# Key-value products of two batches in one group, with k read as loaded, in a fused attention and feed-forward kernel

## The chip, the core and the metric

The kernel runs on one core of a Trainium2 chip. The metric is the device time of one execution in microseconds (us), as the median of several runs. Beside it stands one profiled execution, whose trace gives the start and length of every instruction on the engines (PE for matrix products, PEld for its weight loads, DVE for vector work, ACT for scalar work, POOL and SP, which here mostly issue transfers) and the traffic of the core's 16 DMA engines.

## What is computed

Eight batches of eight heads, 576 tokens each, head width 64. The first half is linear attention without a softmax, with a norm per token and head; the second a feed-forward layer over all 4608 tokens with a PReLU between two products. Cut to its core:

```python
kv  = np.einsum('bhsd,bhse->bhde', k, v)
out = np.einsum('bhsd,bhde->bhse', q, kv)
rms = np.sqrt(np.mean(out * out, axis=-1, keepdims=True) + 1e-06)
x   = (out / rms * g_norm)            # to [4608, 512]
h = x @ w_in                          # [512, 2048]
g = np.maximum(h, 0.0) + alpha * np.minimum(h, 0.0)
return (g @ w_out)                    # [2048, 512]
```

The change is in `kv`: for each batch and head the 64 x 64 product of k and v, summed over the 576 tokens.

## The kernel before

The 4608 tokens are worked through in nine windows of 512 (W = 512, NW = 9). A batch has 576 tokens, so a window and a batch do not coincide: window 4 needs the end of batch 3 and the start of batch 4. The order of instructions on PE, ACT, DVE, POOL and SP is written out by hand; every engine takes its instructions in that order.

The loop at line 1056 runs over w from 1 to 8, and in it over 16 units u. One unit issues the four products of one 128-column block of the feed-forward layer for window w (`m1_group`, line 523; the group of u = 0 is split by `m1_cols` into the first 384 tokens and the last 128 for w >= 3), seven products of the second layer for window w - 1 (`prod_mm`, line 656), and a step of the attention for window w + 1 (`attention`, line 1032). So the attention of a window runs one window ahead of its use.

What the attention of window w + 1 consists of, from w = 2 on: `row_kv` (line 994) makes the key-value products of batch w + 1, at u = 2 for w = 2 and at u = 0 later, as 4 head pairs x 5 token groups x 2 heads = 40 small products into `kv_ps`, and two ACT casts put them into `kv_masked`. `rows_mm` (line 439), one unit later, multiplies the transposed q (`qt_sb`) by `kv_masked`. Then square, sum, root and norm follow for four blocks of 128 tokens (ACT, DVE), and after each norm SP issues a DMA transpose of the 128 normed tokens into `xt` (line 492), the feed-forward input of the next window. The norms of the four blocks come at u = 5, 7, 9, 12 for w = 2 and at u = 3, 6, 8, 11 later. SP also issues five DMA transposes per batch for q (`dma_t`, line 356, into `qt_sb`), at u = 8, 10, 12 or 7, 9, 11.

The loads of k, v and q turn fp32 in memory into fp16 on the core. They are issued by POOL, in one queue. Tokens 0 to 511 of a batch go into stage tiles (`load_main`, line 165, for k and v; `load_q`, line 173), with two stage tiles each for k and v in turn; the last 64 tokens go straight into `bufs` (`load_rem`, line 185), with three of those for k and v. `load_gated(w + 2)` (line 204) stands at the start of each w up to 5 and issues nine loads for batch w + 2: q rest, k rest, k, four for q, v rest, v. The batch is used one w later. The first of them, q rest, waits on POOL until the last DMA transpose of the batch before has read the buffer that it overwrites. Behind the loads in POOL's queue stand stores of finished output (line 550).

The products read v as it was loaded, `stages[b, "v"][:, head, t, :]`, but k from `bufs`, where `regroup` (line 191) has copied it from [head, token group, d] into [token group, head, d]. For batches 4 to 7 ACT does it, in four pieces at u = 9, 11, 13, 15 (`REG_AT`), and for batch 3 in two ACT pieces and one DVE piece at w = 2, u = 0.

`row_tile` (line 72) hands out two tiles of two PSUM banks each in turn, which `kv_ps` and the two `or_ps` of a window share.

Of the kernel before, what the change touches and what calls it, by code (L numbers as in the profile page):

```python
# [10 lines left out]
FP16 = mybir.dt.float16  # L11
# [6 lines left out]
def kernel(  # L18
# [11 lines left out]
    nc = tc.nc  # L30

    B, H, S, D = q.shape
# [3 lines left out]
    P = 128  # L36
    NPAIR = H // 2
# [3 lines left out]
    TPP = S // P  # L41
    MAIN = TPP * P
    REM = S - MAIN
    NT = TPP + 1
# [27 lines left out]
    def row_tile(shape, name):  # L72
        if not row_pool:
            early.close()
            row_pool.append(
                ctx.enter_context(tc.tile_pool(name="psr", bufs=2, space=bass.MemoryType.PSUM))
            )
        t = row_pool[0].tile([P, 2, W], FP32, name=name, tag="r")
        n = 1
        for x in shape:  # L80
            n *= x
        flat = t[:].rearrange("p b n -> p (b n)")[:, 0:n]
        names = [f"x{i}" for i in range(len(shape))]
        return flat.rearrange(
            f"p ({' '.join(names)}) -> p {' '.join(names)}", **dict(zip(names, shape))
        )
# [78 lines left out]
    def load_main(b, nm, h0=0, h1=H):  # L165
        if (b, nm) not in stages:
            stages[b, nm] = stage_p.tile([P, H, TPP, D], FP16, name=f"{nm}st", tag=f"{nm}st")
        nc.gpsimd.dma_start(
            out=stages[b, nm][:, h0:h1].rearrange("p h t d -> p h (t d)"),
            in_=srcs[nm][b, h0:h1, 0:MAIN, :].rearrange("h (p t) d -> p h (t d)", t=TPP),  # L170
        )
# [10 lines left out]
    def buf_of(b, nm):  # L182
        return bufs[min(b, B_NAT) % 2 if nm == "q" else b % NBUF][nm]

    def load_rem(b, nm):
        nc.gpsimd.dma_start(
            out=buf_of(b, nm)[0:REM, 0 if nm == "v" else TPP, :, :],
            in_=srcs[nm][b, :, MAIN:S, :].rearrange("h s d -> s h d"),
        )

    def regroup(b, nm, h0, h1, eng=None):
        dst = buf_of(b, nm)[:, 0:TPP, h0:h1, :].rearrange("p t h d -> p h t d")
        src = stages[b, nm][:, h0:h1, :, :]
        if eng is nc.scalar:
            nc.scalar.copy(out=dst, in_=src)
        else:
            (eng or nc.vector).tensor_copy(out=dst, in_=src)
# [6 lines left out]
    def load_gated(b):  # L204
        load_rem(b, "q")
        if b == B_NAT:
            load_q(b)
        load_rem(b, "k")
        load_main(b, "k")
        if b > B_NAT:  # L210
            load_q(b)
        load_rem(b, "v")
        load_main(b, "v")

    def regroup0(nm, j, n=1):
        i, h = divmod(2 * j, HH)
# [1 line left out]
            out=bufs[0][nm][0:P0, :, 2 * j : 2 * (j + n), :].rearrange("p t h d -> p h t d"),  # L218
            in_=stages[0, nm, i][0:P0, h : h + 2 * n],
        )  # L220

    def regroup_pair(b, nm, j):
        regroup(b, nm, 2 * j, 2 * j + 2, nc.scalar)


    WQ = 4
    w_in_sb = []
# [72 lines left out]


    qts, kvs, xts = {}, {}, {}
    kv_masked = [const_p.tile([P, NPAIR, P], FP16, name=f"kv_masked{i}") for i in range(2)]

    def rows(b):
        return P0 if b == 0 else P
# [1 line left out]
    def n_runs(b):  # L308
        return T0 if b == 0 else NT

    def pair_cols(b, nm, j):
        def f(t):
            n = rows(b)
            if nm == "v" and b == 0:
                h = 2 * j % HH
                return stages[b, nm, 2 * j // HH][0:n, h : h + 2, t, :]
            if nm == "v" and t < TPP:
                return stages[b, nm][:, 2 * j : 2 * j + 2, t, :]
            if nm == "v":
                return buf_of(b, nm)[0:n, 0, 2 * j : 2 * j + 2, :]  # L320
            return buf_of(b, nm)[0:n, t, 2 * j : 2 * j + 2, :]
        return f
# [44 lines left out]
    def step_kv(b, j, pool=(ps_s, "s")):  # L367
        ks, vs = pair_cols(b, "k", j), pair_cols(b, "v", j)
        kv_ps = pool[0].tile([P, P], FP32, name="kv_ps", tag=pool[1])
        for t in range(n_runs(b)):  # L370
            nc.tensor.matmul(  # L371
                out=kv_ps[:],
                lhsT=ks(t),
                rhs=vs(t),
                start=(t == 0),
                stop=(t == n_runs(b) - 1),
            )
        kvs[b, j] = kv_masked[b % 2][:, j, :]
        nc.vector.tensor_mul(out=kvs[b, j], in0=kv_ps[:], in1=mask32[:])


# [609 lines left out]
            ATT_1.setdefault(at, []).append((what, j))  # L991
    ATT = {"t": step_t, "kv": step_kv, "ot": step_ot, "ssq": step_ssq}

    def row_kv(b):
        kv_ps = row_tile([NPAIR, D], "kv_ps")
        for j in range(NPAIR):
            ks, vs = pair_cols(b, "k", j), pair_cols(b, "v", j)
            for t in range(n_runs(b)):
                for i in range(2):
                    rows_i = slice(i * D, (i + 1) * D)  # L1000
                    nc.tensor.matmul(  # L1001
                        out=kv_ps[rows_i, j, :], lhsT=ks(t)[:, i, :], rhs=vs(t)[:, i, :],
                        start=(t == 0), stop=(t == n_runs(b) - 1), skip_group_check=True,
                    )
        for i in range(2):
            rows_i = slice(i * D, (i + 1) * D)
            nc.scalar.copy(out=kv_masked[b % 2][rows_i, :, rows_i], in_=kv_ps[rows_i, :, :])
        for j in range(NPAIR):
            kvs[b, j] = kv_masked[b % 2][:, j, :]

    ATT_ROW = {}
    ROW_AT = {
        True: dict(
# [18 lines left out]
    def attention(w, u):  # L1032
        if W_ROW <= w < NW:
            for what, j in ATT_ROW[w == W_ROW].get(u, ()):
                if what != "kv":
                    ROWS[what](w, j)
                elif w < B:
                    row_kv(w)
            if w + 1 < B:
                dma_t(w + 1, QT_AT[w == W_ROW].get(u, ()))  # L1040
        elif w < NW:
            for what, j in (ATT_1 if w == 2 else ATT_AT).get(u, ()):
                if what == "t" and w >= B_NAT:
                    continue
                if w < B or what in ("ot", "ssq"):
                    if w == 2 and what in ("kv", "ssq"):
                        pool = Q_POOL if j % 2 == 0 else S_POOL
                        (step_kv if what == "kv" else step_ssq)(w, j, pool)
                    else:
                        ATT[what](w, j)  # L1050

    REG_AT = {9 + 2 * j: (("k", j),) for j in range(NPAIR)}

    Y3_AT = [(13, 13), (13, 13), (13, 13), (13, 14), (14, 14), (14, 15), (15, 15), (15, 15), (15, 15), (15, 15), (15, 15), (15, 15), (15, 15), (15, 15), (15, 16), (16, 16)]

    for w in range(1, NW):
        if w + 2 < B:
            load_gated(w + 2)
        for u in range(NF):
            if w >= W_ROW - 1 and u in R_FIRST:  # L1060
                y_read(w - 1, R_FIRST[u])
            late = w >= W_ROW and u == 0
            if late:
                h_ps = h_bank()
                m1_cols(h_ps, w, G_ORDER[u], 0, W - P)
            else:
                m1_group(w, G_ORDER[u])
            if w < 3 and (w, u) in ((1, NF - 1), (2, 0)):
                s_sum(1, w, 2)
            if w == W_ROW - 1:  # L1070
                scale_w_in(G_ORDER[u])
            if w > 1:
                unit_sums(w, u)
            if w == 1 and u == 1:
                regroup(2, "k", 0, H)
            if w == 2 and u == 0:
                h_tags[0] = ("h1", "h2")
                h_turn[0] = 0
            if w > 2 and u == 0 and not late:
                y_read(w - 2, "c12")  # L1080
            if w == 1:
                for i in range(*Y3_AT[u]):
                    y_mm(ys[3], 0, 3, i)
                    if i == NF - 1:
                        y_out(ys[3], 0, 3)
            else:
                for i in range(u * PER, (u + 1) * PER):
                    prod_mm(w - 1, *Y_LIST[i])
                    if late and i == 3:
                        m1_cols(h_ps, w, G_ORDER[u], W - P, W)  # L1090
                        y_read(w - 2, "c12")
                        m1_evac(h_ps, w, G_ORDER[u])
                for what in (R_ROW if w >= W_ROW - 1 else Y_READS).get(u, ()):
                    y_read(w - 1, what)
            attention(w + 1, u)
            if w == 1 and u == 12:
                dma_t(3, (3, 4, 0, 1, 2))
            if w == 1:
                for k in {5: (0,), 7: (1,)}.get(u, ()):
                    s_sum(1, 1, k)  # L1100
                    s_sum(1, 2, k)
            if w + 2 < B:
                for nm, j in REG_AT.get(u, ()) if w > 1 else ():
                    regroup_pair(w + 2, nm, j)
            if w == 2:
                if u == 0:
                    regroup_pair(3, "k", 0)
                    regroup_pair(3, "k", 1)
                    regroup(3, "k", HH, H)
    w = NW - 1  # L1110
    store_engines[0] = (nc.sync, nc.scalar)
    Y_READS[13] = Y_READS.pop(14)
# [54 lines left out]
```

## Time and profile before

| | |
|---|---|
| median of 3 runs | 274.97 us (273.76 to 275.08) |
| the profiled execution | 275.59 us |
| its span in the trace | 273.6 us |
| mean granted TensorE clock | 0.994 |
| PE busy | 266.3 us, 97% of the span |
| DVE busy | 227.9 us, 83% |
| ACT busy | 155.9 us, 57% |
| POOL busy | 86.2 us, 32% |
| software DMA queue (POOL's), share of 16 engines | 69.5% |
| hardware DMA queue (SP's transposes and stores), share | 17.1% |

The span is cut in the page into 40 slices of 6.84 us. A digit there is the busy share of a slice in tenths, where 9 stands for 90% or more. The time from issue to landing of a transfer is measured from the start of the instruction that issues it.

### The profile page before, as it was taken

The numbers are of one execution on the slowest core, as the hardware profiler recorded it, in microseconds if no ns is written. First come the engines' busy times: TensorE is split into PE (matmuls) and PEld (weight loads), VectorE is DVE, ScalarE is ACT, GpSimd is POOL, SyncE is SP. The second block draws the span as 40 slices with busy tenths as digits, with TensorE's granted clock in tenths as the row PEclk, the third lists the DMA queues.
The fourth block names the chain that finished last, engine by engine and source line by source line (L and its number), as shares of the span: only waits on it lengthen the run. The fifth ranks groups of instructions, "written<-read, shape, count | busy, mean of one in ns | idle before, by whom it ended". The sixth has DMA issues, their size and how long they took to land.

```text
span 273.6 us, 5687 instructions
## 1 busy us (share of the span) xinstructions
PE 266.3 (97%) x2181; PEld 170.8 (62%) x2181; DVE 227.9 (83%) x432; ACT 155.9 (57%) x294; POOL 86.2 (32%) x123
## 2 busy tenths in 40 slices
PE   7799999999999999999999999999999999999995
PEld 2364464555666766666666666666666666666794
DVE  6459938899889979997999799979998999877863
ACT  3267555879989865645565556555544553443210
POOL 8773462780733355226421551100110012000200
PEclk9799999999999999999999999999999999999999
DMA  8999999999999689966996699720222122201223
GB/s 161 196 200 199 197 202 189 220 112 162 137 164 180 99 129 149 170 153 113 155 167 147 112 156 164 151 89 19 77 60 77 22 77 60 77 1 41 77 79 116
DMA packets 87343, 34.56 MB, mean 126 GB/s; under 512 B 58884, under 2 KB 85652, under 8 KB 87316
## 3 DMA queue, kind: packets, MB, share of 16 engines
q0 software_dynamic: 58064, 24.35, 69.5%
q1 hardware_dynamic: 28212, 8.83, 17.1%
q10 hardware_dynamic: 1040, 1.02, 1.2%
q8 instruction: 17, 0.28, 0.4%
q14 instruction: 10, 0.08, 0.1%
HBM read 36.71 MB, written 9.44 MB: 169 GB/s over the span
## 4 chain that ended last, share of the span: by engine, by line
PE 95%; DMA 2%; DVE 1%; issue 0%; ACT 0%; POOLq 0%
PE h_ps L507 43%; PE yY L688 15%; PE yX L688 10%; PE yZ L688 10%; PE y L539 5%; DMA vst<-in_v_dram 2%; PE h_ps L530 2%; PE kv_ps L371 2%; PE or_ps L452 1%; PE kv_ps L1001 1%; PE ssq_ps L416 1%; PE qt_ps L327 1%; PE ot_ps L393 1%; PE yZ L683 1%; PE warm_ps L295 0%
## 5 line engine op out<-in xcount | busy, mean ns | idle before, releaser
L507 PE MATMUL h_ps<-xt,w_in_sb 128*128 128x512 f16 x544 | 136.9, 379 | 0.0
L514 ACT ACTIVATE m_sb<-h_ps 128x512 f32<-128x512 f32 x144 | 86.1, 599 | 78.1 <-PE h_ps L507 67.7
L518 DVE SCALAR_TENSOR_TENSOR gt<-m_sb,beta_sb,h_ps 128x512 f16<-128x512 f32 x144 | 106.2, 744 | 24.1 <-ACT m_sb L514 22.5
L507 PEld LDWEIGHTS <-w_in_sb 128*128 128x128 f16 x544 | 52.1, 98 | 40.0
L550 POOL DMA_DIRECT2D out_dram<-y_sb x36 | 22.6, 630 | 134.3 <-ACT y_sb L726 53.4
L688 PEld LDWEIGHTS <-s 128*128 128x128 f16 x496 | 48.5, 98 | 19.1
L688 PEld LDWEIGHTS <-gt 128*128 128x128 f16 x384 | 37.3, 98 | 14.0
L688 PE MATMUL yY<-wsum,s 128*128 128x256 f16 x256 | 36.3, 273 | 0.0
L688 PE MATMUL yX<-w_out_sb,gt 128*128 128x256 f16 x256 | 36.1, 273 | 0.0
L177 POOL DMA_DIRECT2D qst<-in_q_dram x20 | 17.7, 923 | 1.8 <-DMA vst<-in_v_dram 1.8
L688 PE MATMUL yY<-wsum,gt 128*128 128x256 f16 x128 | 17.6, 273 | 0.0
L688 PE MATMUL yZ<-wsum,s 128*128 128x256 f16 x120 | 16.7, 273 | 0.0
L688 PE MATMUL yZ<-w_out_sb,s 128*128 128x256 f16 x120 | 16.7, 273 | 0.0
L487 DVE TENSOR_TENSOR x_rows<-or_ps,rstd_r 128x512 f16<-128x512 f32 x24 | 16.4, 683 | 0.0
L469 DVE TENSOR_REDUCE ssq_r<-sq_sb 128x8 f32<-128x512 f16 x24 | 16.3, 678 | 0.0
L463 ACT ACTIVATE sq_sb<-or_ps 128x512 f16<-128x512 f32 x24 | 14.4, 599 | 2.6 <-PE or_ps L452 2.6
L539 PE MATMUL y<-w_out_sb,gt 128*128 128x512 f16 x64 | 15.8, 379 | 0.0
L625 DVE TENSOR_TENSOR s<-s,gt 128x512 f16<-128x512 f16 x32 | 13.5, 421 | 0.5
L623 DVE TENSOR_TENSOR s<-gt 128x512 f16<-128x512 f16 x32 | 13.4, 418 | 0.0
L629 DVE TENSOR_TENSOR s<-gt,s 128x512 f16<-128x512 f16 x32 | 13.2, 417 | 0.0
L627 DVE TENSOR_TENSOR s<-gt 128x512 f16<-128x512 f16 x32 | 13.0, 418 | 0.0
L720 DVE TENSOR_TENSOR u<-yY,p 128x512 f32<-128x512 f32 x16 | 10.9, 683 | 1.9 <-PE yY L688 1.7
(88 smaller groups left out, 249.9 us busy)
## 6 DMA issues: line engine op xcount, KB each, us to landing
out_dram<-y_sb POOLq DMA_DIRECT2D x16, 256.0 KB, 2.7
kst<-in_k_dram POOLq DMA_DIRECT2D x7, 512.0 KB, 7.9
vst<-in_v_dram POOLq DMA_DIRECT2D x6, 512.0 KB, 10.5
qst<-in_q_dram POOLq DMA_DIRECT2D x20, 128.0 KB, 8.0
w_out_sb<-in_moe_w_out_dram POOLq DMA_DIRECT2D x8, 256.0 KB, 11.7
out_dram<-y_sb SPq DMA_DIRECT2D x5, 256.0 KB, 2.2
w_in_sb<-in_moe_w_in_dram POOLq DMA_DIRECT2D x2, 512.0 KB, 10.0
qst<-in_q_dram POOLq DMA_DIRECT2D x2, 512.0 KB, 12.1
```

Of the source, the lines that this page charges most:

```text
L177: nc.gpsimd.dma_start(out=st[:, t, :, :], in_=srcs["q"][b, :, t * P : (t + 1) * P, :].rearrange("h p d -> p h d"),)
L463: nc.scalar.activation(out=sq[:], in_=o_ps, func=AF.Square)
L469: nc.vector.tensor_reduce(out=ssq[:].rearrange("p h j -> p (h j)"), in_=sq[:].rearrange("p h j d -> p (h j) d"), axis=mybir.AxisListType.X ...
L487: nc.vector.tensor_tensor(out=xr[:].rearrange("p j h d -> p h j d"), in0=o_ps, in1=rstd[:].unsqueeze(3).to_broadcast([P, 2, NPAIR, D]), op ...
L507: nc.tensor.matmul(out=h_ps[:], lhsT=w_in_blk(c, g), rhs=xts[w][:, c, :], start=(c == 0), stop=(c == NC - 1),)
L514: nc.scalar.activation(out=m_sb[:], in_=h_ps[:], func=AF.Relu, scale=-1.0)
L518: nc.vector.scalar_tensor_tensor(out=gts[w, i][:, r, :], in0=m_sb[:], scalar=beta_sb[:, g : g + 1], in1=h_ps[:], op0=ALU.mult, op1=ALU.add,)
L539: nc.tensor.matmul(out=y[:], lhsT=gt_cols(w, g, a * P, (a + 1) * P), rhs=w_out_blk(g), start=(g == 0), stop=(g == NF - 1),)
L550: engs[store_turn[0] % len(engs)].dma_start(out=dst, in_=src)
L623: nc.vector.tensor_add(out=t[:], in0=a21, in1=a22)
L625: nc.vector.tensor_sub(out=t[:], in0=sums[w, 1, k][:], in1=a11)
L688: nc.tensor.matmul(out=bank, lhsT=lhs, rhs=rhs, start=fresh, stop=(c == NK - 1), skip_group_check=True,)
```

## The change

Batch 3 stays alone; batches 4 and 5 are made in one group of 80 products, with one pair of casts, where batch 4 was made alone, and 6 and 7 likewise where batch 6 was. The k and v loads of batch 5 move from the start of w = 3 to the start of w = 2, behind those of batch 4, and those of batch 7 from w = 5 to w = 4, behind those of batch 6; the q loads stay where they are. For batches 3 to 7 the products read k from the stage tile, and the copies go. `kv_masked` has three batch slots in place of two tiles.

```diff
@@ load_gated
         load_rem(b, "q")
         if b == B_NAT:
             load_q(b)
-        load_rem(b, "k")
-        load_main(b, "k")
+        first, *more = {3: (3,), 4: (4, 5), 6: (6, 7)}.get(b, (None,))
+        if first:
+            load_rem(b, "k")
+            load_main(b, "k")
         if b > B_NAT:
             load_q(b)
-        load_rem(b, "v")
-        load_main(b, "v")
+        if first:
+            load_rem(b, "v")
+            load_main(b, "v")
+        for c in more:
+            for nm in ("k", "v"):
+                load_rem(c, nm)
+                load_main(c, nm)
@@
-    def regroup_pair(b, nm, j):
-        regroup(b, nm, 2 * j, 2 * j + 2, nc.scalar)
@@
-    kv_masked = [const_p.tile([P, NPAIR, P], FP16, name=f"kv_masked{i}") for i in range(2)]
+    kv_masked = const_p.tile([P, NBUF, NPAIR, P], FP16, name="kv_masked")
@@ step_kv
-        kvs[b, j] = kv_masked[b % 2][:, j, :]
+        kvs[b, j] = kv_masked[:, b % NBUF, j, :]
@@
-    def row_kv(b):
-        kv_ps = row_tile([NPAIR, D], "kv_ps")
-        for j in range(NPAIR):
-            ks, vs = pair_cols(b, "k", j), pair_cols(b, "v", j)
-            for t in range(n_runs(b)):
-                for i in range(2):
-                    rows_i = slice(i * D, (i + 1) * D)
-                    nc.tensor.matmul(
-                        out=kv_ps[rows_i, j, :], lhsT=ks(t)[:, i, :], rhs=vs(t)[:, i, :],
-                        start=(t == 0), stop=(t == n_runs(b) - 1), skip_group_check=True,
-                    )
+    def head_rows(b, nm, h, t):
+        if t < TPP:
+            return stages[b, nm][:, h, t, :]
+        return buf_of(b, nm)[:, t if nm == "k" else 0, h, :]
+
+    def row_kv(bs):
+        n = len(bs)
+        kv_ps = row_tile([n, NPAIR, D], "kv_ps")
+        for x, b in enumerate(bs):
+            for j in range(NPAIR):
+                for t in range(NT):
+                    for i in range(2):
+                        nc.tensor.matmul(
+                            out=kv_ps[i * D : (i + 1) * D, x, j, :],
+                            lhsT=head_rows(b, "k", 2 * j + i, t),
+                            rhs=head_rows(b, "v", 2 * j + i, t),
+                            start=(t == 0), stop=(t == NT - 1), skip_group_check=True,
+                        )
+                kvs[b, j] = kv_masked[:, b % NBUF, j, :]
+        b0 = bs[0] % NBUF
         for i in range(2):
-            rows_i = slice(i * D, (i + 1) * D)
-            nc.scalar.copy(out=kv_masked[b % 2][rows_i, :, rows_i], in_=kv_ps[rows_i, :, :])
-        for j in range(NPAIR):
-            kvs[b, j] = kv_masked[b % 2][:, j, :]
-
+            part = slice(i * D, (i + 1) * D)
+            nc.scalar.copy(out=kv_masked[part, b0 : b0 + n, :, part], in_=kv_ps[part])
+
+    KV_OF = {3: (3,), 4: (4, 5), 6: (6, 7)}
@@ attention
-                elif w < B:
-                    row_kv(w)
+                elif w in KV_OF:
+                    row_kv(KV_OF[w])
@@ the loop over w
-    REG_AT = {9 + 2 * j: (("k", j),) for j in range(NPAIR)}
...
-            if w + 2 < B:
-                for nm, j in REG_AT.get(u, ()) if w > 1 else ():
-                    regroup_pair(w + 2, nm, j)
-            if w == 2:
-                if u == 0:
-                    regroup_pair(3, "k", 0)
-                    regroup_pair(3, "k", 1)
-                    regroup(3, "k", HH, H)
```

## The prediction

> **What bounds the kernel now.** I read the page's engine shares and its chain of work first, to see which engine sets the end.
>
> ```profile
> PE 266.3 (97%) x2181; PEld 170.8 (62%) x2181; DVE 227.9 (83%) x432; ACT 155.9 (57%) x294; POOL 86.2 (32%) x123
> ...
> PE 95%; DMA 2%; DVE 1%; issue 0%; ACT 0%; POOLq 0%
> ```
>
> The chain that ends last is PE's own work for 95% of the span. Its DMA part (2%) is the wait for v of batch 0 that ends near 8 us; the change does not touch it. Next I asked whether PE runs dense in the stretch that the change touches. The timeline of PE at the turn from w = 2 to w = 3, and below it the turn from w = 6 to w = 7, where there are no key-value products left to make (columns: start us, length us, engine, line, operation, out<-in, shape, count):
>
> ```profile
> 94.48 0.81 PE L530 MATMUL h_ps<-xt,w_in_sb 128*128 128x384 f16 x4
> 95.13 0.60 PE L688 MATMUL yX<-w_out_sb,gt 128*128 128x256 f16 x4
> 95.56 0.39 PE L530 MATMUL h_ps<-xt,w_in_sb 128*128 128x128 f16 x4
> 95.79 0.49 PE L688 MATMUL yX<-w_out_sb,gt 128*128 128x256 f16 x3
> 96.21 0.32 PE L1001 MATMUL kv_ps<-vst,ksb 128*64 128x64 f16 x8
> 96.36 0.20 PE L1001 MATMUL kv_ps<-vsb,ksb 128*64 128x64 f16 x2
> ...
> 96.67 0.20 PE L1001 MATMUL kv_ps<-vsb,ksb 128*64 128x64 f16 x2
> ...
> 96.96 1.04 PE L507 MATMUL h_ps<-xt,w_in_sb 128*128 128x512 f16 x4
> ```
>
> ```profile
> 206.15 0.39 PE L530 MATMUL h_ps<-xt,w_in_sb 128*128 128x128 f16 x4
> 206.37 0.49 PE L688 MATMUL yX<-w_out_sb,gt 128*128 128x256 f16 x3
> 206.70 1.03 PE L507 MATMUL h_ps<-xt,w_in_sb 128*128 128x512 f16 x4
> ```
>
> In the chain a unit is four products of 0.86 us together and seven of 0.77 us: 1.63 us, sixteen of them 26.0 us. The windows that start at 97.03, 124.62, 152.32, 179.91 and 206.86 us last 27.6, 27.7, 27.6, 26.9 and 26.7 us: the units, the small attention products, and no gap. So nothing that ACT or DVE gives up can shorten these windows, and whatever makes PE wait lengthens the run by as much. There are two inputs that PE could wait for here: the normed tokens in `xt` (needed at 94.48 and 95.56 us) and k and v (needed at 96.21).
>
> **What the change takes off PE.** The products stay 200 in number, with the same operand shapes. The second pair ends at 96.36 + 0.20, the next a step of 0.155 us later (96.36, 96.51, 96.67), so 40 products stream in 4 x 0.155 = 0.62 us. From the last 128-column products to the next group PE takes 96.96 - 95.56 = 1.40 us with key-value products and 206.70 - 206.15 = 0.55 us without: a group costs 0.85 us, of which 0.85 - 0.62 = 0.23 us is entry and exit. Two groups fewer (those of batches 5 and 7): 2 x 0.23 = **0.46 us gained**. Bounds: nothing, if the streams do not pack as well, and 0.5.
>
> **What it takes off ACT and DVE.** 18 copies (line 195) of 611 ns, 10.9 us on ACT, and one DVE copy of 418 ns. ACT is idle for 78.1 us ahead of its own line 514 alone, mostly waiting for PE; in this stretch PE never waits for ACT. Worth **0**. If that slack were not there, the four copies of one window would be worth 2.4 us.
>
> **What it adds on ACT.** The casts of one batch take 0.37 us each (line 1007); those of two batches have twice the elements. The step from 128x256 to 128x512 in the squares (382 to 595 ns) puts 256 elements at 0.21 us, so 0.58 each and 1.16 the pair. Before, they ended at 97.82 and `rows_mm` began at 98.70. With 0.62 us more products, the casts end near 97.08 + 0.62 + 1.16 = 98.86 and `rows_mm` would begin at 99.32: hidden with 0.46 us to spare. **0**; a cover gone would cost what it is late, at most a few tenths.
>
> **What it moves: four loads.** On POOL the issues at the start of w = 2 are:
>
> ```profile
> 70.20 0.69 POOL L186 DMA_DIRECT2D qsb<-in_q_dram  x1 [9.81 <-DMA qt_sb<-qsb]
> 70.88 0.70 POOL L186 DMA_DIRECT2D ksb<-in_k_dram  x1
> 71.56 0.91 POOL L168 DMA_DIRECT2D kst<-in_k_dram  x1
> 72.43 3.54 POOL L177 DMA_DIRECT2D qst<-in_q_dram  x4
> 75.89 0.76 POOL L186 DMA_DIRECT2D vsb<-in_v_dram  x1
> 76.57 0.97 POOL L168 DMA_DIRECT2D vst<-in_v_dram  x1
> 82.85 2.16 POOL L550 DMA_DIRECT2D out_dram<-y_sb  x4 [5.32 <-ACT rstd_r L479]
> ```
>
> Behind the issue at 76.57 come k rest, k, v rest, v of batch 5: 0.70 + 0.91 + 0.76 + 0.97 = 3.3 us of issuing. At the start of the kernel POOL issued eight loads and then waited for the first to land (1.14 us, at 8.27), so the new k load waits for the third load of this batch, which lands at 71.56 + 8.4 = 79.96, and the new v load for the second q load, near 81.6. All are in the queue before v of batch 4 lands (76.57 + 10.7 = 87.27), so the DMA engines do not run dry. The stage tiles that they overwrite, of batch 3, are free at 72.5, where its products end. POOL's stores of 82.85 land later; there are four `y_sb` tiles and four are filled per window, so each has 27 us. Issuing: **0**. The later windows lose these loads, where they were hidden anyway: **0**.
>
> The transfers themselves are another matter. Between the landing of k (79.96) and that of v (87.27) the queue brought four q loads, v rest and v: 4 x 128 + 64 + 512 KB = 1.11 MB in 7.3 us, 152 GB/s. Two k and v pairs of the moved batch are 1152 KB = 1.18 MB: 7.8 us more, until 95.0, and in this time three transposes of 128 KB also want the engines (0.13 MB at 152 GB/s is 0.86 us each), 97.6 at the outside. PE needs batch 5 at 96.21 + 0.62 = 96.8. Late by **0 to 0.8 us**. At w = 4 v of batch 6 lands at 132.20 + 10.7 = 142.9; batch 7 then at 150.7 to 153.3, needed at 151.50 + 0.62 = 152.1: **0 to 1.2 us**.
>
> **What is late next: the transposes into `xt`.** They share the 16 engines with the loads. Transfers by issue, in narrow stretches, one at 109.19 while the loads of w = 3 fill the engines and one at 91.90 after those of w = 2 are through (SP's queue, microseconds to landing last):
>
> ```profile
> xt<-x_rows SPq DMA_TRANSPOSE x1, 7.8
> ```
>
> ```profile
> xt<-x_rows SPq DMA_TRANSPOSE x1, 2.5
> ```
>
> In the stretch from 78 to 82 us every digit of DMA use is 9, and the one transpose issued there (80.25) has moved no bytes by 83. So a transpose under load takes up to 7.8 us, and 2.5 without. The fourth block of w = 2 is issued at 91.90 and needed at 95.56: 94.4 without load, 99.7 at worst with it. The load lasts until some 95 to 97.6, that is for most of the flight; I take 5.5 us, a little above the middle, hence 97.4: **1.8 us late** (bounds 0 and 4.1). The kv group then begins 1.8 later and the load of batch 5 is there. The third block (issued 86.69) lands by 94.5 even at 7.8, when it is needed at 94.48. At w = 4 the fourth block is issued at 145.03 and needed at 150.85: 5.8 us of room, so late only above that (bounds 0 and 2.0); I take the load of batch 7 as the later one there, **1.0 us**, near its far bound, since transposes and loads lengthen each other.
>
> The Trainium skill's page "DMA: Bandwidth & Descriptors", section "Queues, rings and completion order", says that each DMA engine goes round robin between the queues that have work, packet by packet. By that rule a transpose would have half the engines' rate at once: 0.13 MB at half of 152 GB/s, 1.7 us in place of 0.9, some 3.4 us to landing as an estimate, and both blocks would be in time; the sum would be -0.46 us or little above. The row of 7.8 us speaks against so even a share, so I go by the row.
>
> **The sum.** -0.46 + 1.8 + 1.0 = +2.34 us on the profiled execution's 275.59 (a span of 273.6 and 2.0 around it): 277.9. The median of the runs shown is 0.6 below that execution, so 277.3 for the median. Bounds: -0.46, and -0.46 + 4.1 + 2.0 = +5.6.
>
> **The rivals.** *All of it is hidden.* The place is the same, the fourth block's transpose and the moved loads. For it: v loads alone ran at 195 to 209 GB/s (82 to 84 us), and between 84 and 96 us the engines were idle for some 6.2 us by the digits of their use. At 200 GB/s the load takes 5.9 us and is through at 93.2; a transpose that lands within 3.7 us of its issue at 91.90, and 5.8 at 145.03, costs nothing. Then only the 0.46 us remains: 274.97 - 0.46 = 274.5, not slower. It decides from that 3.7 us. Against it: those issued while the engines were full took 5.2 to 7.8 us. *A backlog.* Transposes go through one queue in order; at w = 4 those issued at 136.90, 138.18, 140.15 and 141.44 all landed between 144.1 and 145.8, some 3 us after the loads of that window were through at about 142. If that repeats behind a load that lasts until 97.6, the third block of w = 2 lands at 100.6, 6.1 us after 94.48, and w = 4 adds 2.0: with the 0.46 off, +7.6, 282.6. For it: that bunching. Against it: under load the ones of 132.01 and 109.19 came through in 7.1 and 7.8 us, before the load ended. *The pairing helps PE more than I count*, by over 0.5%: that needs 1.4 us off PE, three times the entry and exit of both groups; I see no row for it.
>
> **How the numbers follow.** About 0.5%, 1.4 us, is what a measurement of this kernel can tell from no change. Forecast (late by 1.4 to 5.6 us): 0.50, its own range 276.3 to 280.6. All hidden or nearly: 0.37. Backlog: 0.10. More gain: 0.03. So slower 0.60, same 0.37, faster 0.03. The range has to take in the hidden case: 274.2 to 280.6, which leaves out the backlog and little below.
>
> **What would show it.** In the trace after: PE idle ahead of line 530 at w = 3, u = 0 (about 1.8 us, released by the transpose into `xt`), and ahead of the kv group at w = 5 (about 1 us, released by the load into the v or k stage tile); transposes issued near 92 and 145 us with landings of 5 us and more; the software queue at full use until about 95 and 151 us; two kv groups of about 1.45 us and none at two window starts; windows of 26.7 us without. I am wrong if PE has no gaps there, if line 452 waits for the casts, or if the gap is over 4 us.

## The result

| | before | after |
|---|---|---|
| median of 6 runs each | 274.68 us (273.76 to 275.37) | 289.11 us (286.86 to 290.06) |
| ratio, with its 95% interval | | 1.052 (1.047 to 1.056) |
| the profiled execution, its span | 275.59, 273.6 us | 289.28, 287.4 us |
| mean granted TensorE clock | 0.994 | 0.976 |

The change costs 14.4 us, where 2.3 was forecast. One of the experiments below (one pair, even loads) has runs in two groups 4 us apart; they are given one by one there.

The page of the changed kernel, engine shares, the slices of PE and its clock, and the chain of work that ended last:

```profile
PE 269.5 (94%) x2181; PEld 172.7 (60%) x2181; DVE 228.1 (79%) x431; ACT 146.6 (51%) x272; POOL 86.5 (30%) x123
...
PE   7799999999999399999998299999999999999995
...
PEclk9999999999999869999999699999999999999999
...
PE 87%; DMA 7%; DVE 3%; ACT 1%; issue 1%; DVEq 0%
```

Two slices of PE now read 3 and 2 (a slice is 7.2 us here). The clock reads 8 in the first of them and 6 in the slice behind it, and 6 in the second. DMA's part of the chain has risen from 2% to 7%; the page's list by line gives nearly all of it to `xt<-x_rows`, SP's transposes. The PE timeline at the two turns (lines are 3 higher than before at `m1_cols`, so 533 is the old 530; in brackets the idle time ahead and what ended it):

```profile
94.59 0.81 PE L533 MATMUL h_ps<-xt,w_in_sb 128*128 128x384 f16 x4 [1.46 <-DMA xt<-x_rows]
...
99.47 0.58 PE L533 MATMUL h_ps<-xt,w_in_sb 128*128 128x128 f16 x4 [3.63 <-DMA xt<-x_rows]
99.85 0.84 PE L691 MATMUL yX<-w_out_sb,gt 128*128 128x256 f16 x3
100.62 0.43 PE L1009 MATMUL kv_ps<-vst,kst 128*64 128x64 f16 x8
100.86 0.25 PE L1009 MATMUL kv_ps<-vsb,ksb 128*64 128x64 f16 x2
100.91 0.41 PE L1009 MATMUL kv_ps<-vst,kst 128*64 128x64 f16 x8
...
157.01 0.82 PE L533 MATMUL h_ps<-xt,w_in_sb 128*128 128x384 f16 x4 [0.94 <-DMA xt<-x_rows]
...
163.69 0.59 PE L533 MATMUL h_ps<-xt,w_in_sb 128*128 128x128 f16 x4 [5.41 <-DMA xt<-x_rows]
```

PE waits for the first three blocks (1.46 and 0.94 us) and again for the fourth (3.63 and 5.41): 5.1 us at the first turn, 6.35 at the second, all of it released by a transpose into `xt`. Line 1009 has no idle time ahead of it: PE does not wait for k or v. But its pairs of heads come 100.91 - 100.62 = 0.29 and then 0.27 us apart, where it was 0.155 before. The granted clock by stretches of 2 us shows why (columns: PE, PEld, DVE, ACT, POOL busy with instructions, then the clock, DMA share, GB/s):

```profile
96.00:98.00 2.00, 0.00 (x0) 0.00 (x0) 0.00 (x0) 0.00 (x0) 0.68 (x2) 1.00 1.29 212
98.00:100.00 2.00, 0.53 (x5) 0.53 (x5) 0.00 (x0) 0.00 (x0) 0.00 (x0) 0.57 1.31 114
100.00:102.00 2.00, 2.00 (x56) 1.52 (x55) 0.75 (x1) 0.60 (x1) 0.60 (x1) 0.50 1.35 135
102.00:104.00 2.00, 2.00 (x41) 1.27 (x36) 0.00 (x0) 0.98 (x2) 0.33 (x1) 0.50 0.78 268
104.00:106.00 2.00, 2.00 (x29) 1.19 (x29) 0.54 (x1) 0.78 (x2) 1.52 (x3) 0.73 0.52 33
106.00:108.00 2.00, 2.00 (x36) 1.40 (x29) 0.90 (x4) 1.25 (x3) 2.00 (x3) 1.00 1.14 73
```

During the wait the clock falls to half, and it stays there for 5.6 us after PE is at work again (until 105.10), at the second turn for 2.9 us (163.69 to 166.54). The wait is paid once more in slow products.

And the transfers, asked for by issue, for the fourth blocks' transposes (issued at 90.40 and 151.18 us):

```profile
xt<-x_rows SPq DMA_TRANSPOSE x1, 9.0
...
xt<-x_rows SPq DMA_TRANSPOSE x1, 12.5
```

9.0 and 12.5 us from issue to landing, where they took 2.5 and 3.2 before. They are not issued later than before: 17.68 and 18.75 us after the first `rows_mm` of their window, to the hundredth as in the kernel before. So ACT and DVE, which make the blocks, are in time, and the transfers are late. The loads of v that run beside them (issued at 82.61 for batch 5 and at 143.53 for batch 7) take

```profile
vst<-in_v_dram POOLq DMA_DIRECT2D x1, 512.0 KB, 17.4
...
vst<-in_v_dram POOLq DMA_DIRECT2D x1, 512.0 KB, 19.3
```

against 10.7 us for the v loads of batches 4 and 6 before.

To lay the kernels side by side, free of the first 70 us, which vary by up to 1.5 us between executions, I take the starts of `rows_mm` in the PE timeline (line 452, later 455): the time from the one of w = 2 to that of w = 3, then to w = 4, then to w = 5.

| kernel | w = 2 to 3, us | 3 to 4 | 4 to 5 |
|---|---|---|---|
| before | 24.48 | 27.58 | 27.71 |
| after | 32.98 | 26.73 | 36.20 |
| k as loaded only | 24.48 | 27.58 | 27.70 |
| loads moved too, no groups | 32.54 | 27.58 | 34.68 |
| batch 6 loaded a window earlier | 32.13 | 26.73 | 28.33 |
| only k moved, no groups (277.41 us) | 25.59 | 27.58 | 29.42 |
| q's transposes last | 30.77 | 26.73 | 32.25 |
| PE kept busy | 30.07 | 26.73 | 34.20 |
| q's transposes left out | 27.06 | 26.73 | 30.19 |
| one pair, loads even (280.61 us) | 24.47 | 28.83 | 33.07 |

A group of two batches puts 40 more products, 0.62 us, into the interval that it opens, the first or the third. Without them the changed kernel loses 32.98 - 24.48 - 0.62 = 7.9 us at the first turn and 36.20 - 27.71 - 0.62 = 7.9 at the second, and gains 27.58 - 26.73 - 0.62 = 0.23 us where a group has gone, twice. Of the two losses PE's waits are 5.1 and 6.35 us. The rest, 2.8 and 1.5, is the slow clock: 5.6 and 2.9 us of work at half of it cost half of these times.

### The profile page after: what moved, and what is told of

The parts are those of the page before. It is cut to its first block, busy times and chain, and to the rows that moved or that the text cites. A ratio compares the mean times of both kernels' runs of the same rounds, so it can differ in the third digit from the quotient of the medians.

```text
span 287.4 us, 5664 instructions
## 1 busy us (share of the span) xinstructions
PE 269.5 (94%) x2181; PEld 172.7 (60%) x2181; DVE 228.1 (79%) x431; ACT 146.6 (51%) x272; POOL 86.5 (30%) x123
## 4 chain that ended last, share of the span: by engine, by line
PE 87%; DMA 7%; DVE 3%; ACT 1%; issue 1%; DVEq 0%
PE h_ps L510 39%; PE yY L691 13%; PE yX L691 10%; PE yZ L691 8%; DMA xt<-x_rows 7%; PE y L542 5%; PE warm_ps L298 2%; PE kv_ps L1009 2%; PE h_ps L533 2%; PE kv_ps L374 1%; PE or_ps L455 1%; PE qt_ps L330 1%; PE ssq_ps L419 1%; PE ot_ps L396 1%; PE yZ L686 1%
## 5 line engine op out<-in xcount | busy, mean ns | idle before, releaser
L691 PE MATMUL yX<-w_out_sb,gt 128*128 128x256 f16 x256 | 37.1, 277 | 0.0
L533 PE MATMUL h_ps<-xt,w_in_sb 128*128 128x384 f16 (+1 forms) x48 | 7.6, 286 | 11.4 <-DMA xt<-x_rows 11.4
L472 DVE TENSOR_REDUCE ssq_r<-sq_sb 128x8 f32<-128x512 f16 x24 | 16.3, 678 | 0.0
L542 PE MATMUL y<-w_out_sb,gt 128*128 128x512 f16 x64 | 15.9, 379 | 0.0
L466 ACT ACTIVATE sq_sb<-or_ps 128x512 f16<-128x512 f32 x24 | 14.4, 599 | 2.6 <-PE or_ps L455 2.5
L626 DVE TENSOR_TENSOR s<-gt 128x512 f16<-128x512 f16 x32 | 13.4, 418 | 0.0
```

Source lines behind the costliest of these rows:

```text
L466: nc.scalar.activation(out=sq[:], in_=o_ps, func=AF.Square)
L472: nc.vector.tensor_reduce(out=ssq[:].rearrange("p h j -> p (h j)"), in_=sq[:].rearrange("p h j d -> p (h j) d"), axis=mybir.AxisListType.X ...
L542: nc.tensor.matmul(out=y[:], lhsT=gt_cols(w, g, a * P, (a + 1) * P), rhs=w_out_blk(g), start=(g == 0), stop=(g == NF - 1),)
L626: nc.vector.tensor_add(out=t[:], in0=a21, in1=a22)
L691: nc.tensor.matmul(out=bank, lhsT=lhs, rhs=rhs, start=fresh, stop=(c == NK - 1), skip_group_check=True,)
```

## The experiments

The theory under test: the moved loads and SP's transposes share the DMA engines, `xt` comes late, and PE, which has no slack, waits. The diffs are against the changed kernel.

**The parts one by one.** First only the reading of k as loaded, then the loads too, while the groups come last (the changed kernel itself).

```diff
-        first, *more = {3: (3,), 4: (4, 5), 6: (6, 7)}.get(b, (None,))
+        first, *more = (b,)
-    KV_OF = {3: (3,), 4: (4, 5), 6: (6, 7)}
+    KV_OF = {b: (b,) for b in range(3, B)}
```

> Only the reading of k as loaded and the three slots of kv_masked remain; products, casts and loads batch by batch, as before. Theory (the moved loads hold up the transposes into xt): no change, 274.7 us, at most 0.3% either way, since ACT and DVE work hidden behind PE is all that goes. Rival (reading k from the stage tile costs PE or moves a wait): slower, up to the whole 289.

Measured: 274.47 us in the median of 11 runs, ratio 0.9994 (0.9981 to 1.0007). No wait for `xt`, and the three intervals of the table are those of before. ACT's busy time falls from 155.9 to 147.2 us and moves nothing, and reading k as loaded costs nothing.

With the second of the two edits alone, the loads go where the change puts them and each batch keeps its own products:

> As the first, and the k and v loads of batches 5 and 7 moved ahead as in the change; every batch still has its own products at its own window, so nothing waits early for k and v of batch 5 or 7. Theory: all of the loss is here, 287 to 290 us, PE idle ahead of line 533 at both turns, about 5 and 6 us, released by the transpose into xt. Rival (the group of 80 products, its casts or its wait for v): near 275.

Measured: 289.78 us (286.50 to 291.46), ratio 1.049 (1.043 to 1.055). The loss is here in full, without a single group. The waits are of the size that they have in the changed kernel, except that PE does not wait for the first three blocks of the second turn:

```profile
94.80 0.81 PE L533 MATMUL h_ps<-xt,w_in_sb 128*128 128x384 f16 x4 [1.24 <-DMA xt<-x_rows]
...
100.27 0.58 PE L533 MATMUL h_ps<-xt,w_in_sb 128*128 128x128 f16 x4 [4.23 <-DMA xt<-x_rows]
...
163.32 0.59 PE L533 MATMUL h_ps<-xt,w_in_sb 128*128 128x128 f16 x4 [5.32 <-DMA xt<-x_rows]
```

The rival that the groups, their casts or an early need of k and v cost the time falls: none of them is in this kernel.

**Both groups, the second window evened out.** k and v of batch 6 are loaded one window earlier, where only q of batch 5 was left.

```diff
-        first, *more = {3: (3,), 4: (4, 5), 6: (6, 7)}.get(b, (None,))
+        first = b in (3, 4)
...
-        for c in more:
+        for c in {4: (5,), 5: (6,), 6: (7,)}.get(b, ()):
```

> The change with both groups, but k and v of batch 6 loaded at w = 3 beside q of batch 5, and k and v of batch 7 at w = 4 beside q of batch 6: three tensors in each of these windows, as before the change; w = 2 keeps five. Theory: the second stall goes, the first stays, 281 to 283 us, no PE gap at the turn to w = 5. Rival (the groups): 289.

Measured: 281.46 us (280.85 to 282.14), ratio 1.025 (1.023 to 1.027). The first turn still loses 32.13 - 24.48 - 0.62 = 7.0 us, the second nothing at all: 28.33 us is 27.71 + 0.62. The group of batches 6 and 7 runs at 0.16 us per pair and no gap stands ahead of it. So the group as such is harmless, and half of the loss hangs on the loads of one window.

**Half the bytes.** As the second experiment, with only k of batches 5 and 7 moved.

```diff
-        first, *more = {3: (3,), 4: (4, 5), 6: (6, 7)}.get(b, (None,))
+        first = b not in (5, 7)
+        more = {4: (5,), 6: (7,)}.get(b, ())
...
-        if first:
-            load_rem(b, "v")
-            load_main(b, "v")
+        load_rem(b, "v")
+        load_main(b, "v")
...
-            for nm in ("k", "v"):
-                load_rem(c, nm)
-                load_main(c, nm)
+            load_rem(c, "k")
+            load_main(c, "k")
```

> As the second, but only k of batches 5 and 7 moved ahead (0.59 MB more in w = 2 and w = 4 in place of 1.18). Theory: the loads last some 5 us less long, and the transpose of the fourth block lands earlier by about that: 276 to 280 us, most of the loss gone, as PE had 3.7 and 5.8 us of room before. If the loss goes with the bytes in proportion: 282. Rival (the groups): 275.

Measured: 275.98 us (275.16 to 277.41), ratio 1.006 (1.004 to 1.008), just below the span expected, and far from a share by bytes (282). In the profiled execution, of 277.41 us, the waits for `xt` are 0.63 and 0.16 us at the first turn and 1.53 at the second; the fourth blocks land 4.7 and 7.0 us after their issue at 90.90 and 145.15. The clock does not fall: its mean is 1.000. The loss is not in proportion to the bytes: by the medians the first 0.59 MB in each of the two windows cost 1.3 us, the next 0.59 MB some 14.

**The order on SP.** The transposes of q that stand between the four blocks go behind them.

```diff
-    QT_AT = {False: {7: (0,), 9: (1,), 11: (2, 3, 4)}, True: {8: (0,), 10: (1,), 12: (2, 3, 4)}}
+    QT_AT = {False: {12: (0,), 13: (1,), 14: (2, 3, 4)}, True: {13: (0,), 14: (1,), 15: (2, 3, 4)}}
```

> The change, with the DMA transposes of q issued behind the fourth block's transpose into xt (u = 13 to 15 at w = 2, u = 12 to 14 later) in place of between the blocks. Theory that transposes come through one behind another, at the share that the loads leave: two transposes fewer, 0.26 MB, stand ahead of the fourth block's; at the 0.06 MB per us that this queue got beside the loads that is some 4 us, so the fourth block lands 3 to 4 us sooner and the time falls to 280 to 285 us, unless the products of line 455 then wait for q. Rival (each transpose is held until the loads are through, whatever stands ahead of it): the fourth block lands near 99 us as before, 288 us or more.

Measured: 283.58 us (280.29 to 284.82), ratio 1.026 (1.021 to 1.031), in the span of the theory; but the two turns do not say the same. Line 455 waits for no q. PE waits 0.53 us for the first three blocks of the first turn, and for the fourth blocks

```profile
99.17 0.38 PE L533 MATMUL h_ps<-xt,w_in_sb 128*128 128x128 f16 x4 [3.33 <-DMA xt<-x_rows]
...
158.32 0.58 PE L533 MATMUL h_ps<-xt,w_in_sb 128*128 128x128 f16 x4 [2.44 <-DMA xt<-x_rows]
```

The fourth block of the second turn lands 8.38 us after its issue in place of 12.46, the 4 us expected. That of the first takes 7.80 in place of 9.03: only 1.2. For the first turn alone this leaves the question open, hence the next experiment.

**No transposes of q beside the moved loads.** Those of batches 4 and 6 are left out.

```diff
-                dma_t(w + 1, QT_AT[w == W_ROW].get(u, ()))
+                ts = QT_AT[w == W_ROW].get(u, ())
+                dma_t(w + 1, () if w + 1 in (4, 6) else ts)
```

> The change without the DMA transposes of q for batches 4 and 6 (left out: the products of line 455 read old columns there, so the output of the windows with these batches is not the reference's). Beside the moved loads SP then sends only the four blocks into xt, 0.5 MB in place of 1.1. Theory (loads and transposes share the engines and lengthen each other, one transpose behind another): the loads of batches 5 and 7 land 2 to 4 us sooner after their issue than 17.4 and 19.3 us, the fourth block lands 4 to 6 us after its issue in place of 9.0 and 12.5, and the time falls to 276 to 281 us. Rival (the loads alone hold each transpose until they are through): the fourth block lands with the load of v, 7 us or more after its issue, 283 us or more.

Measured: 278.10 us (277.45 to 278.52), ratio 1.012 (1.009 to 1.015). PE's waits shrink to 0.45 us for the first three blocks of the first turn and, for the fourth blocks, to

```profile
97.17 0.38 PE L533 MATMUL h_ps<-xt,w_in_sb 128*128 128x128 f16 x4 [1.17 <-DMA xt<-x_rows]
...
154.10 0.38 PE L533 MATMUL h_ps<-xt,w_in_sb 128*128 128x128 f16 x4 [1.70 <-DMA xt<-x_rows]
```

The loads of v of batches 5 and 7 land sooner after their issue:

```profile
vst<-in_v_dram POOLq DMA_DIRECT2D x1, 512.0 KB, 13.8
...
vst<-in_v_dram POOLq DMA_DIRECT2D x1, 512.0 KB, 15.3
```

The changed kernel has 17.4 and 19.3 there; in the profiles of the three others that move the same loads into w = 2 and keep q's transposes between the blocks, the first takes 15.9 to 16.3. The fourth block of the first turn lands 5.6 us after its issue (8.6 to 9.4 in those four kernels), that of the second after 7.7 (146.42 to 154.10, above the 4 to 6 expected) in place of 12.5. So the loads get faster when transposes go, and the transposes that are left get faster too: each lengthens the other.

The rival, loads that hold each transpose until they are through, does not give this time: 278 us, not 283 or more. The changed kernel's own trace speaks against it too. Three transposes ahead of the first turn's fourth block land there at 90.4, 91.7 and 94.5 us, while the load of v lasts until 100.0. But the fourth block itself lands close to the end of the loads in every profile in which both k and v are moved into its window: from 0.6 us before the last load (99.4 against 100.0, the change, first turn) to 2.8 after it (163.3 against 160.5, the loads without groups, second turn); here at 97.1 against 95.2, and both at 154.1.

**PE kept busy in the wait.** Products that nothing reads fill the long waits, so that only the wait itself is left.

```diff
+    FILL = {3: 16, 5: 24}
...
                     if late and i == 3:
+                        if w in (3, 5):
+                            fill = row_tile([W], "fill_ps")
+                            for n in range(FILL[w]):
+                                nc.tensor.matmul(
+                                    out=fill, lhsT=ident16[:], rhs=w_out_sb[0][:, 0, :],
+                                    start=True, stop=True,
+                                )
```

> The change, with 16 and 24 products into an unused PSUM tile ahead of the second part of line 533 at w = 3 and w = 5, so that PE is busy in most of the two long waits (3.6 and 5.4 us); the tile is read by nothing. Theory (after the waits PE runs at half its clock for some 6 us, which costs 2 to 3 us each on top of the waits): the clock stays at 1.0 and the time falls to 283 to 286 us, though PE does more. Rival (the products after the wait are slow because of the transfers): 289 us or more.

Measured: 284.75, 284.80, 287.15 and 293.57 us. The first three, with a clock of 1.000, give the ratio 1.040 (1.036 to 1.044), and two of them lie in the span expected; the clock of the fourth is 0.988, and no profile of it shows why it is longer. PE does 40 products more, and the three are 2 to 4 us faster than the changed kernel's median of 289.11. The timeline around the first turn:

```profile
95.71 3.62 PE L1104 MATMUL fill_ps<-w_out_sb,ident 128*128 128x512 f16 x16
99.42 0.38 PE L533 MATMUL h_ps<-xt,w_in_sb 128*128 128x128 f16 x4
...
100.06 0.32 PE L1009 MATMUL kv_ps<-vst,kst 128*64 128x64 f16 x8
...
100.24 0.29 PE L1009 MATMUL kv_ps<-vst,kst 128*64 128x64 f16 x8
...
101.45 1.04 PE L510 MATMUL h_ps<-xt,w_in_sb 128*128 128x512 f16 x4
```

The fourth block comes at the same time (99.4), but the pairs behind it are 0.16 us apart, and the clock of the whole run is 1.000. So the rival, that the transfers slow the products, falls. By the table this kernel is 32.98 - 30.07 = 2.9 us faster at the first turn and 36.20 - 34.20 = 2.0 at the second. The first is the slow clock's 2.8; at the second the fourth block also landed 0.8 us sooner after its issue than in the changed kernel (11.65 against 12.47), so the clock's 1.5 there is the better figure. This kernel also shows what a group saves at full clock: from the 128-column products to the next `h_ps` it takes 101.45 - 99.42 = 2.03 us with 80 products; a batch alone took 1.40 and a turn without products 0.55. So 2 x 1.40 - 2.03 - 0.55 = 0.22 us per pair.

**One pair, loads even.** The smallest form of the change that might gain: only 6 and 7 as a group, and four tensors in each of two windows.

```diff
-        first, *more = {3: (3,), 4: (4, 5), 6: (6, 7)}.get(b, (None,))
-        if first:
+        if b < 6:
             load_rem(b, "k")
...
-        if first:
+        if b < 7:
             load_rem(b, "v")
...
-        for c in more:
-            for nm in ("k", "v"):
-                load_rem(c, nm)
-                load_main(c, nm)
+        for c, nm in {5: ((6, "k"),), 6: ((7, "k"), (7, "v"))}.get(b, ()):
+            load_rem(c, nm)
+            load_main(c, nm)
...
-    KV_OF = {3: (3,), 4: (4, 5), 6: (6, 7)}
+    KV_OF = {3: (3,), 4: (4,), 5: (5,), 6: (6, 7)}
```

> k read as loaded, batches 3, 4, 5 alone and 6 and 7 in one group; k of batch 6 loaded at w = 3 behind batch 5, k and v of batch 7 at w = 4 behind q and v of batch 6: four tensors in each of these windows in place of three. Theory: PE gains the 0.2 us of one group and loses what four tensors in a window cost; half the moved bytes left gaps of 0.8 and 1.5 us, so 274.3 to 277 us. Rival (the group itself costs): over 278.

Measured: 276.29, 276.43, 276.88 and 280.61, 280.68, 281.85 us. The first three give the ratio 1.007 (1.005 to 1.009) and are in the span expected; the others are not, so it is a miss in half of the runs. The profiled execution is that of 280.61 us:

```profile
151.56 0.82 PE L531 MATMUL h_ps<-xt,w_in_sb 128*128 128x384 f16 x4 [1.11 <-DMA xt<-x_rows]
154.72 0.58 PE L531 MATMUL h_ps<-xt,w_in_sb 128*128 128x128 f16 x4 [1.90 <-DMA xt<-x_rows]
155.88 0.42 PE L1007 MATMUL kv_ps<-vst,kst 128*64 128x64 f16 x8
...
156.17 0.40 PE L1007 MATMUL kv_ps<-vst,kst 128*64 128x64 f16 x8
```

Here too `xt` is late, and the pairs behind are 0.29 us apart: the clock is down. The mean clock on record is 0.998 to 1.000 in the three faster runs and 0.987 to 0.992 in the slower ones, so in the faster it stayed up. That is not all of their difference of 4 us: at this turn the profiled execution loses 33.07 - 27.71 - 0.62 = 4.7 us, of which 3.0 are waits and 1.7 the clock. The waits of a faster run were not profiled. The window with k of batch 6 as its fourth tensor loses 28.83 - 27.58 = 1.25 us. No version tried beats the kernel before; a group is worth 0.22 us at best, and a fourth tensor in a window costs more.

## Why the prediction was wrong

The direction was right, the place too at the first turn, and so was the absence of slack on PE. The size was off by a factor of six, and the time lay above the range. Two terms of the sum failed. The lateness of PE's inputs, put at 1.8 + 1.0 us with bounds of 4.1 and 2.0, measured 5.1 + 6.35. The price of a wait beyond the wait itself, put at nothing without a word, measured 2.8 + 1.5 us of slow clock. The prediction's own sign of being wrong, a gap over 4 us, came at both turns. Step by step:

- *Two groups fewer: 0.46 us gained.* Right: 0.23 us twice by the table, 0.22 by the group at full clock.
- *Copies, casts, POOL's issuing: nothing.* Right. The first experiment has the copies' part; the two casts of a pair take 1.17 us, and line 455 waits for none; the k load of batch 5 waits 2.2 us on POOL, until 81.06, with the third load landing at 72.17 + 8.4 = 80.6, as foreseen, and it does not matter.
- *"A transpose under load takes up to 7.8 us."* This step failed. I took the longest landing seen as a bound. It was only the longest for the three tensors a window then had, and I misread it: the block issued at 109.19 landed at 117.0, after the load of v beside it (115.9), not before its end. With five tensors a transpose stands behind more of its own kind and beside loads that last longer: 9.0 and 12.5 us, with waits of 5.1 and 6.35 us where I had 1.8 and 1.0. Counted from the first `rows_mm` of w = 2, the fourth block was to land after 23.2 us and after 25.5 at worst (97.4 and 99.7 less 74.22); it landed after 26.7, and after 26.3 to 27.1 in the three other profiles with these loads and these transposes.
- *"152 GB/s: 7.8 us more ... three transposes of 128 KB."* The rate was near, the bytes too few. After v of batch 4 has landed (77.18 + 11.4 = 88.6) until v of batch 5 has (100.0) the queues moved, in packets, MB and share of 16 engines:

```profile
q0 software_dynamic: 1951, 1.06, 73.4%
q1 hardware_dynamic: 3136, 0.76, 70.8%
```

  The two add up to 1.82 MB in 11.4 us, 160 GB/s, where I had 1.57 MB at 152. Of them 0.76 MB are transposes: a block alone shows as 542 packets and 0.13 MB, so 3136 packets are six blocks' worth and not three. I counted those issued in the stretch; of the five issued before it, 0.65 MB, only 0.24 MB had moved by 88.6. At the second turn, from 149.4 to 162.8, the two queues moved 2.17 MB, 162 GB/s, where I had 7.8 to 10.4 us of traffic and it took 13.4.
- *When the loads start.* The loads of w = 2 began 4.0 us ahead of the first `rows_mm` in the profile that I read (70.20 and 74.22) and 1.9 ahead in the changed kernel's (70.81 and 72.72). The other profiles have 1.9 to 4.0, and the kernel with one pair, which moves nothing in that window, has 1.9: so this is a spread between executions that I took for fixed, and not the moved loads. It decides little, for the loads without groups (2.4) and batch 6 loaded earlier (2.7) lose 8.1 and 7.0 us at the first turn, the change 7.9.
- *The second wait put down to the load of batch 7.* Wrong: the load lands at 162.8, before the fourth block (163.6), and it is the block that PE waits for; line 1009 has no idle time. The loads were late as well, only hidden by that. Without a wait for the fourth block the products of batches 5 and 7 would have come near 97.1 and 159.5 (the end of PE's work at 95.84 and 158.28, and 0.65 + 0.62 us of products as before), as an estimate; v landed 2.9 and 3.3 us after that, where I had 0 to 0.8 and 0 to 1.2.
- *The Trainium skill's rule.* I set "DMA: Bandwidth & Descriptors", "Queues, rings and completion order" (engines go round robin between queues, packet by packet) against the row of 7.8 us and followed the row. In the microsecond from 152 to 153 the changed kernel shows:

```profile
q0 software_dynamic: 265, 0.09, 84.7%
q1 hardware_dynamic: 264, 0.07, 59.5%
```

  These are packets in equal numbers, and from 87 to 96 us there are 2122 and 2081: in these stretches the trace agrees. From 145 to 147, with the transposes issued at 143.04 and 144.34 still to land, it does not:

```profile
q0 software_dynamic: 935, 0.36, 166.3%
q1 hardware_dynamic: 18, 0.00, 2.7%
```

  No run here shows why. My estimate of 3.4 us by the rule left out two things: the loads last longer by what the transposes take (the experiment without q's transposes), and a packet's turn says nothing of how many packets of the same queue stand ahead. So a long landing and an even share are no contradiction.
- *Left out altogether: the clock.* 2.8 and 1.5 us, over a quarter of the loss, came from products at half clock behind the waits. I asked what each wait costs and not what PE is like after it.
- *The rivals.* The backlog, at 0.10, was nearest: the third block was late too, as it says, though by 1.5 and 0.9 us and not 6, and the fourth by more. Its 282.6 with the clock's 4.3 added would have been 286.9, still short. Its condition was misread as well: the load of w = 4 was through at 142.9, not at about 142, so the bunched transposes landed 1.2 to 2.8 us behind it and not some 3. All hidden is out.

The sum as measured, from the table: 7.9 + 7.9 - 0.46 = 15.3 us; the medians differ by 14.4, the spans of the two profiled executions by 13.8, since the one before reached its first `rows_mm` 1.5 us later.

What stays open: why a transpose issued while the loads fill the engines moves nothing for its first 3 to 4 us (before: issued 80.25, nothing by 83; the change: 78.75 and 83, 138.16 and 142), and why the second turn's fourth block took 12.5 us against the first's 9.0 with as many tensors in its window. Most of that difference goes with the transposes of q (8.4 and 7.8 us with them behind, 7.7 and 5.6 without them), but why they weigh more there is not shown.

## What to carry to other kernels

When loads move to an earlier window, add up all bytes of all queues that share the DMA engines in that window, those still waiting there included, and hold the sum against the deadline of the last transfer that the busy engine needs; the moved data itself may be in time and something small beside it late. A landing time seen at one load is no bound at a higher one. In the profiles with both k and v moved, the end of the loads was a better guess for the last transpose than any landing seen before. On PE, where it is the bound, a wait of a few microseconds has a second price, the slower clock behind it, to be read in the clock column and kept in the sum.

## What the runs showed of the hardware

- The clock: waits of 0.63 and 0.16 or of 1.53 us (half the bytes), and of 1.70 (q's transposes left out), left it at 1.000; a single wait of 2.44 (q's transposes last, second turn), 1.11 and 1.90 within some 4 us (one pair), or 1.46 and 3.63 (the change), brought it to a half.
- The half clock came in stretches of 3.4 us, one or two of them: 98.27 to 105.10 and 159.71 to 166.54 in the change, 100.03 to 103.44 and 158.05 to 161.47 with q's transposes last, 154.66 to 158.08 with one pair. The first starts during a wait, the stretch at 100.03 only 0.9 us after its wait was over. In the 3.4 us just ahead of each of these starts PE had stood idle for 2.43, 2.15, 2.56, 2.18 and 2.15 us. In the loads without groups 1.94 us of idle in such a stretch (156.53 to 159.94) left the clock at 1.000, and the fall came after the next one. So what counts in these traces is how much of the wait falls into one such stretch, and a wait near 2 us can tip a run. The Trainium skill, "TensorE: Matmul & The Clock Gate", "What's actually happening", has the half clock after an idle window of about 3.4 us; the length agrees, but here 2.15 us of idle, with products between, were enough.
- DMA transposes of 128 KB landed in 2.5 us with the engines free and in 9.0 and 12.5 beside 1.18 MB more of loads, while both queues together moved 160 GB/s (88.6 to 100.0 us) and 162 (149.4 to 162.8).
- The 64 x 64 key-value products stream at 0.155 us per ten, 16 ns each, at full clock, and at 0.27 us per ten, 27 ns each, at half.
